# A retention block and a Strassen feed-forward: where the weight forms, their first sums and v's scaling stand in the queues

## The chip, the cores and the metric

The kernel runs on one core of a Trainium2 chip. The metric is device time in microseconds (us), lower is better. The core has five instruction queues: PE (matmul), DVE (vector), ACT (scalar), POOL (GpSimd) and SP, which here only issues transfers. ACT and POOL issue transfers too. Each queue is worked off in order.

## The reference, cut to what matters

```python
def _attn_ref(q, k, v):            # each (8, 8, 576, 64): batch, heads, sequence, head width
    scores = 1/sqrt(64) * q @ k.T
    rel = pos[:, None] - pos[None, :]
    Dmat = where(rel >= 0, gamma[:, None, None] ** rel, 0.0)   # one gamma per head
    return (scores * Dmat) @ v
...
x = attn_out.transpose(0, 2, 1, 3).reshape(4608, 512)
a = x @ w1                          # 512 -> 1024
b = x @ w2
h = a * b @ w3                      # 1024 -> 1024
out = h @ w_out                     # 1024 -> 512
```

Everything is float32. The weights arrive as float64 and are converted by hand.

## The kernel before, in words

**Attention.** The batch is worked in four pairs (`i`), and the 576 positions of a pair in five chunks, one of 64 and four of 128. So there are 20 chunks, `g` from 0 to 19. For each chunk the kernel loads k (`ld_k`) and v (`ld_v`). From the second pair on it also loads q, and a little later k, in 32 x 32 blocks (`load_blocks`, L171: sixteen transfers of 32 KB for q and sixteen for k, half as many for a short chunk), so that DVE can transpose them (`front_blocks`, L190). POOL multiplies v by the decay (`scale`, L204) and q's blocks by theirs (`scale_blocks`, L181). Then come the scores on PE (`score`, L233), their mask on DVE (L236), the running state (`state`, L255, copied by ACT in L259), and the product with v (`pv`, L274 and L299, copied by ACT into `xT` in L306).

**Feed-forward.** `w3` and `w_out` are multiplied into one matrix `w3o` early on. What remains per token is two products with `w1` and `w2` (`up`), their elementwise product (`ab`), and one product with `w3o` (`down`). Both use Strassen's scheme with seven products for eight. In `up` (L524) and `down` (L637) it is one level deep. A `down` takes two groups of 128 tokens: PE makes products 1, 7, 2, 6, 5, 4 and 3, ACT copies product 1 (L667) and product 2 on top of it (L682), and DVE makes the sums (L681, L641) and the operands S3, S2, S1, S4 (L607, L611, L613, L679). The result tile `ot` has one buffer. Its rows are stored by ACT (L708).

From token block 4 on, `up2` goes one level deeper, for two token blocks at a time (a group; there are four groups of 14 steps, seven for each half of the weights). Each step is one of the seven outer products P1, P2, P6, P7, P4, P5, P3, and makes seven inner products of 0.65 us each. It needs one set of weight forms of 896 KB, which doesn't stay on the chip: the sets are computed once by `weight_forms`, written to HBM (`kept`), and read back step by step into a ring of three slots in `ra` (`next_forms`, L931). A step issues the read for the step after the next. In a step ACT copies three or four results (L1036, L1040, L1043, L1031), POOL adds earlier results to them (`more`, L1022), DVE adds the rest (L1029, L1027), and for every second quarter of the result DVE multiplies the two factors into `ab` (L994). The last inner product of a step (`rest`) is put off into the step after it, behind that step's second product, by `finish`. The token side has sums too: `token_forms` (L940, all on POOL), once per group.

**Handing over the weights.** `wA0`, `wA1` (weights of half 0 and 1) and `wS0`, `wS1` (their sums) fill the space that the ring and the result tiles take over. `weight_forms(h, False)` makes one pair of sums on DVE (L868: one on wA, one on wS) and sends two thirds of the forms; `weight_forms(h, True)` makes three more pairs in place, and sends the rest. One half is 6.4 MB. A send is five transfers per piece (L878 of 256 KB or 128 KB each, L881 or L884 for wS), all issued by POOL. The work of these functions is put in a list, `spread`, from which `up` and `down` take one entry after each of their DVE sums. `open_first` (half 0) and `open_second` (half 1) empty the list and open the ring; `open_second` then issues the first two reads. In the third `down` of this stretch, L667 writes into `ra` as well, in the space of `wA1`.

**Order.** The order on every queue is written out by hand (`manual_schedule`); the framework adds the waits. `work(n)` takes n entries from `todo`, a list of `up`, `up2` and `down`; `aside` holds pieces (transposes, sums) that the next `up` or `down` takes along. The stretch that the change touches first is this:

```python
todo.extend([*ups[:2], forms[0], ups[2], forms[1], ups[3], forms[2], (down, (1, 0), (1, 1)), forms[3],
             (down, (2, 2), (3, 2)), (open_second,), (down, (3, 0), (3, 1))])
```

and the loop that follows it, for chunks 10 to 19, begins with

```python
scale(g + 1, "v")
work(n - 2)
scale_blocks(g + 1)
for nm in "qk":
    aside.append(lambda nm=nm: front_blocks(g + 1, nm))
    work(1)
```

where v of chunk g + 1 was asked for at the end of the turn before, on ACT's queue.

Of the kernel before, what the change touches and what calls it, by code (L numbers as in the profile page):

```python
# [19 lines left out]
def kernel(  # L20
# [13 lines left out]
    nc = tc.nc  # L34
# [590 lines left out]
    def down(x, y, then=None, last=False):  # L625
        a, done, left = pair_of(x, y)
        second = "first" in live
        ahead(x, y)
        while len(done) < (1 if second else 3):
            aside.pop(0)()  # L630
        ps = {}
        ot = pools["ot"].tile([P, 2, 2, DM // 2], F32, tag="ot", name="ot")

        def product(nm, A, B, on=None):
            ps[nm] = ps[on] if on else acc.tile([P, DM // 2], F32, tag="acc", name="po")
            for f in range(NP):
                nc.tensor.matmul(ps[nm], a[A][:, f, :], live["W"][B][:, f, :], start=(f == 0 and not on),  # L637
                                 stop=(f == NP - 1), skip_group_check=True)

        def plus(nm, to, sb):  # L640
            nc.vector.tensor_add(ot[:, to[0], to[1]], ps[nm], ot[:, sb[0], sb[1]])  # L641
            if spread:
                spread.pop(0)()
            if second and aside and nm != 3:
                aside.pop(0)()

        def put(m, t, row, half=slice(0, 2)):

            i, n = every[m]
            r0 = t * P  # L650
            while r0 < (t + 1) * P:
                b = r0 // TB
                e = min((b + 1) * TB, (t + 1) * P)
                r = (2 * i + b) * S + n * TB + r0 - b * TB
                stores.append((out[r:r + e - r0, half.start * DM // 2:half.stop * DM // 2],
                               ot[r0 - t * P:e - t * P, row, half].rearrange("p h d -> p (h d)")))
                r0 = e
            if not keep_stores and not second:
                store()

        C11, C12, C21, C22 = (0, 0), (0, 1), (1, 0), (1, 1)
        product(1, "A11", "B11")
        first = ot[:, 0, 0]
        if second:
            first = live["first"].pop(0)
            live["first"].append(first)
        nc.scalar.copy(first, ps[1])  # L667
        if second:
            store()
            finish()  # L670
        product(7, "S3", "T3")
        if second:
            multiply()
        while len(done) < 3:
            aside.pop(0)()
        if then:
            ahead(*then)
        product(2, "A12", "B21", on=1)
        nc.vector.tensor_tensor(out=a["S4"], in0=a["A12"], in1=a["S2"], op=ALU.subtract)  # L679
        product(6, "S2", "T2")  # L680
        nc.vector.tensor_add(ot[:, 0, 1], ps[6], first)  # L681
        nc.scalar.copy(ot[:, 0, 0], ps[2])  # L682
        plus(7, C21, C12)
        product(5, "S1", "T1")
        plus(5, C22, C21)
        product(4, "A22", "-T4")
        plus(4, C21, C21)
        put(*y, 1)
        if last or second:
            put(*x, 0, slice(0, 1))  # L690
        if second:
            store()
        product(3, "S4", "B22", on=5)
        while aside and not second:
            aside.pop(0)()
        plus(3, C12, C12)
        put(*x, 0, slice(1 if last or second else 0, 2))
        if last:
            store()
        while aside:  # L700
            aside.pop(0)()
# [156 lines left out]

    def weight_forms(h, second):

        wa, ws = wA[h].rearrange("p r j c n -> p (r j) c n"), wS[h]

        def tt(out, in0, in1, op):
            def both():
                for w in (wa, ws):
                    o, x, y = (w[:, :, c, m * QC:(m + 1) * QC] if w is wa else w[:, :, m, :, c, :]
                               for m, c in (out, in0, in1))
                    nc.vector.tensor_tensor(out=o, in0=x, in1=y, op=op)  # L868
            return both

        def send(pieces):
            for lo, m, c in pieces:
                n = 2 * P if c == 1 else 4 * P
                for a in range(4):
                    f, r = divmod(a, 2)
                    x = wA[h][:, r, :, :, m * QC + f * P:m * QC + f * P + P]
                    x = x.rearrange("p j c n -> p (j c) n") if c is None else x[:, :, c, :]
                    nc.gpsimd.dma_start(kept[h][a, :, lo:lo + n].rearrange("p (g n) -> p g n", n=P), x)  # L878
                to = kept[h][4:7, :, lo:lo + n].rearrange("a p n -> p a n")
                if c is None:  # L880
                    nc.gpsimd.dma_start(to, wS[h][:, :, m].rearrange("p a j c n -> p a (j c n)"))  # L881
                else:
                    for j in range(2):
                        nc.gpsimd.dma_start(to[:, :, j * P:(j + 1) * P], wS[h][:, :, m, j, c, :])  # L884

        if second:
            return [tt((1, 1), (1, 1), (1, 0), ALU.subtract), tt((0, 0), (1, 1), (0, 0), ALU.add),
                    tt((0, 1), (0, 1), (1, 1), ALU.subtract),
                    lambda: send([(8 * P, 0, None), (12 * P, 1, 1)])]
        return [tt((1, 0), (0, 0), (1, 0), ALU.subtract), lambda: send([(0, 0, None), (4 * P, 1, None)])]  # L890
# [21 lines left out]
    def open_second():  # L912
        nonlocal acc
        while spread:
            spread.pop(0)()
        acc_part.close()
        acc = ctx.enter_context(tc.tile_pool(name="acc", bufs=5, space=PSUM, reuse_waits="tile"))
        pools["seed"] = ctx.enter_context(tc.tile_pool(name="seed", bufs=2, space=PSUM, reuse_waits="tile"))
        ra = wp.tile([P, 32 * P], F32, tag="wA1", name="ra")
        cs = wp.tile([P, 2, 4, 2, TB], F32, tag="wS1", name="cc")  # L920
        ring.extend([ra[:, :FORM], ra[:, FORM:2 * FORM]])
        free.extend(cs[:, j] for j in range(2))
        live["first"] = [ra[:, 2 * FORM + j * DM // 2:2 * FORM + (j + 1) * DM // 2] for j in range(2)]
        for _ in range(2):
            next_forms()

    def next_forms():
        n = sent[0]
        if n < 14 * len(groups):
            nm = NAMES.index(OPERANDS[order[n % 7]][0])  # L930
            nc.gpsimd.dma_start(ring[n % 3], kept[n % 14 // 7][nm])  # L931
            sent[0] += 1

    def token_forms(gr):
# [5 lines left out]
            nc.gpsimd.tensor_tensor(out=out, in0=in0, in1=in1, op=op)  # L940

        for s in range(2):
            B = [[x[s][:, 2 * r:2 * r + 2, b, :] for b in range(2)] for r in range(2)]
            tt(B[0][1], B[1][1], B[0][1])
            tt(T[:, s, 1], B[0][1], B[0][0], ALU.add)
            tt(T[:, s, 0], B[1][1], T[:, s, 1])
            tt(T[:, s, 2], B[1][0], T[:, s, 1])
        b11, b21 = (x[0].rearrange("p (r c) b t -> p r c b t", c=2)[:, :, c] for c in range(2))
        b12, b22 = (x[1].rearrange("p (r c) b t -> p r c b t", c=2)[:, :, c] for c in range(2))
        tt(b12, b22, b12)  # L950
        tt(E[:, 1], b12, b11, ALU.add)
        tt(E[:, 0], b22, E[:, 1])
# [44 lines left out]
    def up2(gr, n):  # L997
# [41 lines left out]
        product(p5, "S1", "T1", True)  # L1039
        nc.scalar.copy(c[:, 3], p5)  # L1040
        finish()
        product(p6, "S2", "T2")
        nc.scalar.copy(c[:, 1], p6)  # L1043
        for o in both:
# [9 lines left out]
            more(c, add, 1)  # L1054
        for o in both:
            more(o, c, 1)
        next_forms()
        product(p6, "S3", "T3")
        plus(p6, 3, c)
        plus(p5, 1, c)  # L1060
        if both:
            multiply()
        if aside:
            aside.pop(0)()

        def rest():
# [6 lines left out]
            elif key == "P4":  # L1073
                results.append((gr, h, 1, 0, c))
            elif key == "P5":
                free.append(c)
                results.append((gr, h, 1, 1, sums2["P7"]))
            elif key == "P3":
                free.append(sums2["P6"])
# [39 lines left out]
    for g in first_pair:  # L1119
# [28 lines left out]
            scale_blocks(g + 2)  # L1148
        if g == NC + 1:
            list(strassen_tokens(1, 0))  # L1150
            forms = [(lambda h=h, second=second: spread.extend([lambda: None] * (2 * second) + weight_forms(h, second)),)
                     for h in halves for second in (False, True)]
            ups = [(up, 1, 0, fp) for fp in range(NQ)]
            todo.extend([*ups[:2], forms[0], ups[2], forms[1], ups[3], forms[2], (down, (1, 0), (1, 1)), forms[3],
                         (down, (2, 2), (3, 2)), (open_second,), (down, (3, 0), (3, 1))])
        if not in_blocks[g + 1]:
            work(n // 2)
# [9 lines left out]
    scale(g + 1, "v")  # L1167
    open_first()
    rest = token_forms(0)

    g = 2 * NC
    work(1)
# [11 lines left out]
    for g in range(2 * NC, G):  # L1184
        n = dealt[g - 2 * NC]
        if g + 1 < G:
            scale(g + 1, "v")
            work(n - 2)
            scale_blocks(g + 1)
            for nm in "qk":  # L1190
                aside.append(lambda nm=nm: front_blocks(g + 1, nm))
                work(1)
# [64 lines left out]
```

## Time and profile before

| | |
|---|---|
| median of 8 runs | 897.47 us (894.01 to 901.94) |
| the profiled execution | 898.61 us, its span from first to last instruction 896.9 us |
| mean granted PE clock | 0.977 of full speed |
| busy: PE, DVE, POOL, ACT | 829.5, 554.9, 343.5, 257.9 us |
| moved by the transfer engines | 128.77 MB, mean 144 GB/s |
| reads of weight forms (`ra<-kept`) | 56 of 896 KB, median 5.0 us from issue to landing |
| q and k blocks (`bl_q`, `bl_k`) | 408 of 32 KB, median 2.5 us |

Stages, by the timeline: the first pair with the conversion of the weights (to about 200 us), the second pair with `up` and `down` (to 320), the weights sent out between three `down` (320 to 380), then the four groups of `up2`, each followed by three `down` (from 390 to the end).

How to read it: "busy" is an engine's own work. A wait is put down to what ended last before the waiting instruction. `seed` and `up` are accumulators in PSUM; `cc` are the result tiles of the steps; "x4" behind a row of the timeline is a number of instructions merged into it. Each product in float32 shows twice as many matmul records as the code has calls. The timeline's three columns at the left are start, duration (both in us) and engine; a bracket tells the idle time before it and what ended it. In a list of waits the numbers are the sum in us, how often, and the longest.

### The profile page before, as it was taken

The numbers are of one execution on the slowest core, as the hardware profiler recorded it, in microseconds if no ns is written. First come the engines' busy times: TensorE is split into PE (matmuls) and PEld (weight loads), VectorE is DVE, ScalarE is ACT, GpSimd is POOL, SyncE is SP. The second block draws the span as 40 slices with busy tenths as digits, with TensorE's granted clock in tenths as the row PEclk, the third lists the DMA queues.
The fourth block names the chain that finished last, engine by engine and source line by source line (L and its number), as shares of the span: only waits on it lengthen the run. The fifth ranks groups of instructions, "written<-read, shape, count | busy, mean of one in ns | idle before, by whom it ended". The sixth has DMA issues, their size and how long they took to land.

```text
span 896.9 us, 15684 instructions
## 1 busy us (share of the span) xinstructions
PE 829.5 (92%) x6053; PEld 739.7 (82%) x6053; DVE 554.9 (62%) x891; ACT 257.9 (29%) x501; POOL 343.5 (38%) x349
## 2 busy tenths in 40 slices
PE   7999999999999988868988899999899999999998
PEld 6889999446889976767887688888789898898987
DVE  4989899963554665414646933667735759346563
ACT  4786566641111110022321003222013231033200
POOL 1100010002013545964446913647904458534510
PEclk8999999999999998979989999999999999999999
DMA  9994544533255687558786337587546452235401
GB/s 192 218 221 113 90 129 137 141 71 59 48 108 107 130 273 247 172 172 206 169 229 150 78 73 175 206 204 202 92 86 178 151 197 88 85 124 188 164 24 47
DMA packets 234089, 128.77 MB, mean 144 GB/s; under 512 B 203096, under 2 KB 216664, under 8 KB 234016
## 3 DMA queue, kind: packets, MB, share of 16 engines
q1 hardware_dynamic: 188448, 47.52, 27.5%
q0 software_dynamic: 11872, 64.23, 20.7%
q10 hardware_dynamic: 33696, 16.03, 7.7%
q8 instruction: 47, 0.77, 0.4%
q14 instruction: 26, 0.21, 0.1%
HBM read 105.46 MB, written 22.28 MB: 142 GB/s over the span
## 4 chain that ended last, share of the span: by engine, by line
PE 54%; DMA 20%; DVE 8%; POOL 7%; SPq 5%; issue 4%; ACT 1%; ACTq 0%; DVEq 0%; POOLq 0%
PE po L637 19%; PE up L524 9%; PE up L1017 8%; DMA ra<-kept 7%; PE ps L477 6%; PE seed L1017 6%; DMA ld_v<-in_v_dram 5%; SPq L171 4%; DMA bl_k<-in_k_dram 3%; PE sc L233 2%; DMA out_dram<-ot 2%; POOL cc L1022 2%; PE xps L299 2%; DVE ab L994 2%; DVE cc L1029 1%
## 5 line engine op out<-in xcount | busy, mean ns | idle before, releaser
L1022 POOL TENSOR_TENSOR cc<-cc 128x384 f32<-128x384 f32 x112 | 111.8, 1008 | 111.4 <-ACT cc L1040 99.6
L637 PE MATMUL po<-w3o,ab 128*128 128x256 f32 x552 | 126.0, 383 | 5.1 <-DVE ot L641 2.4
L637 PEld LDWEIGHTS po<-w3o,ab 128*128 128x128 f32 x552 | 105.3, 192 | 21.0 <-DVE ot L641 3.4
L1029 DVE TENSOR_TENSOR cc<-seed,cc 128x384 f32<-128x384 f32 x88 | 48.7, 554 | 96.5 <-PE seed L1017 90.4
L204 POOL TENSOR_TENSOR ld_v<-ld_v,gk 128x1024 f32<-128x1024 f32 (+1 forms) x18 | 34.4, 1910 | 182.4 <-DMA ld_v<-in_v_dram 171.7
L1017 PE MATMUL up<-xT,ra 128*128 128x192 f32 x384 | 76.8, 334 | 16.8 <-DMA ra<-kept 14.9
L1017 PEld LDWEIGHTS up<-xT,ra 128*128 128x128 f32 x384 | 63.8, 191 | 22.5 <-issue 10.5
L524 PE MATMUL up<-xT,wA 128*128 128x192 f32 x384 | 70.5, 327 | 0.0
L637 PE MATMUL po<-wB,forms 128*128 128x256 f32 x288 | 66.8, 385 | 3.8 <-DVE forms L611 3.3
L1036 ACT COPY seed<-up 128x384 f32<-128x384 f32 x56 | 25.9, 463 | 152.6 <-PE up L1017 128.5
L1029 DVE TENSOR_TENSOR cc<-up,cc 128x384 f32<-128x384 f32 x88 | 48.3, 549 | 31.6 <-PE up L1017 30.2
L181 POOL TENSOR_TENSOR bl_q<-bl_q,gqs 128x512 f32<-128x512 f32 (+1 forms) x30 | 31.0, 1053 | 95.1 <-DMA bl_q<-in_q_dram 89.7
L1017 PE MATMUL up<-ra 128*128 128x192 f32 x288 | 57.3, 336 | 10.7 <-DMA ra<-kept 10.6
L529 DVE TENSOR_TENSOR c<-up,c 128x384 f32<-128x384 f32 x80 | 44.0, 550 | 36.6 <-PE up L524 36.0
L637 PEld LDWEIGHTS po<-wB,forms 128*128 128x128 f32 x288 | 55.3, 193 | 12.9 <-issue 4.0
L236 DVE TENSOR_TENSOR pm<-sc,mask 128x512 f32<-128x512 f32 (+1 forms) x80 | 45.4, 628 | 31.6 <-PE sc L233 31.6
L524 PEld LDWEIGHTS up<-xT,wA 128*128 128x128 f32 x384 | 63.4, 190 | 1.2 <-issue 0.5
L1017 PEld LDWEIGHTS up<-ra 128*128 128x128 f32 x288 | 48.7, 195 | 13.8 <-DMA ra<-kept 10.4
L477 PE MATMUL ps<-wo,w3T 128*128 128x512 f32 x128 | 55.1, 592 | 0.0
L994 DVE TENSOR_TENSOR ab<-cc 128x384 f32<-128x384 f32 x64 | 54.1, 886 | 0.8
L1017 PE MATMUL seed<-e,ra 128*128 128x192 f32 x256 | 53.0, 339 | 0.5 <-DVE cc L1029 0.4
L679 DVE TENSOR_TENSOR ab<-ab,forms 128x512 f32<-128x512 f32 x17 | 16.8, 988 | 52.6 <-PE po L637 52.6
(126 smaller groups left out, 1553.8 us busy)
## 6 DMA issues: line engine op xcount, KB each, us to landing
ra<-kept POOLq DMA_DIRECT2D x56, 896.0 KB, 5.0
raw<-in_moe_w_dram SPq DMA_DIRECT2D x72, 128.0 KB, 3.0
bl_q<-in_q_dram SPq DMA_DIRECT2D x216, 32.0 KB, 2.5
ld_k<-in_k_dram SPq DMA_DIRECT2D x13, 512.0 KB, 5.3
out_dram<-ot ACTq DMA_DIRECT2D x50, 128.0 KB, 2.3
bl_k<-in_k_dram SPq DMA_DIRECT2D x192, 32.0 KB, 2.5
kept<-wA POOLq DMA_DIRECT2D x24, 256.0 KB, 4.0
ld_v<-in_v_dram ACTq DMA_DIRECT2D x11, 512.0 KB, 6.9
```

The lines of the kernel that those rows point to most:

```text
L171: nc.sync.dma_start(t[part:part + BL, :, m, :], src[a, :, s0:s0 + BL, f * BL:(f + 1) * BL].rearrange("m r x -> r m x"))
L181: nc.gpsimd.tensor_tensor(out=part, in0=part, in1=gqs[:, :, n0:n0 + n].unsqueeze(3).to_broadcast([P, NP, n, BL]), op=ALU.mult)
L204: engine.tensor_tensor(out=t, in0=t, in1=gam[:sz, c].unsqueeze(1).unsqueeze(3).to_broadcast([sz, 2, H, D]), op=ALU.mult)
L236: nc.vector.tensor_mul(pm[:sz, b, j, :, :sz], sc[j][:sz, :, :sz], mask[:sz, :sz].unsqueeze(1).to_broadcast([sz, NP, sz]))
L477: nc.tensor.matmul(ps, live["w3T", ft][:, g, :], live["wo"][:, g, :], start=(g == 0), stop=(g == KF - 1))
L524: nc.tensor.matmul(ps[:, w, :], a[:, w, r, :], b[:, r, :], start=(new and w == r == 0), stop=(w == r == 1), skip_group_check=True)
L529: nc.vector.tensor_add(c[:, to], ps, c[:, sb])
L637: nc.tensor.matmul(ps[nm], a[A][:, f, :], live["W"][B][:, f, :], start=(f == 0 and not on), stop=(f == NP - 1), skip_group_check=True)
L994: nc.vector.tensor_mul(ab, v[:, :, 0, :], v[:, :, 1, :])
L1017: nc.tensor.matmul(ps[:, w, :], weight_of(slot, a, w), B[b], start=(new and w == 0), stop=True, skip_group_check=True)
L1022: nc.gpsimd.tensor_tensor(out=o, in0=o, in1=i, op=ALU.add)
L1029: nc.vector.tensor_add(c[:, j], ps, with_add[:, j])
```

## The change

Six edits. (1) The order of the weight forms: half 0's first sums stay where they are, half 1's first sums and half 0's second sums both come after the last `up`, during the first `down`, and half 1's second sums are put in `spread` behind `token_forms(0)`, so that the second `down` takes them. (2) The sends of half 1's second forms, and the two reads of `open_second`, are issued by SP instead of POOL. (3) In `token_forms` the sums of the two token blocks alternate, with both first sums ahead. (4) `next_forms` moves in a step from behind POOL's adds to directly behind `finish()`. (5) The P5 step gives its own tile `c` back before `multiply`, and not in its `rest`. (6) In the loop v is scaled behind q's blocks; and in one `down` (g == 2 * NC - 1) the first half of a row is stored before product 3, as is done later on.

```diff
@@ down
-        if last or second:
+        early = second or last or g == 2 * NC - 1
+        if early:
             put(*x, 0, slice(0, 1))
...
-        put(*x, 0, slice(1 if last or second else 0, 2))
+        put(*x, 0, slice(1 if early else 0, 2))
@@ weight_forms
+        engine = nc.sync if h and second else nc.gpsimd
...
-                    nc.gpsimd.dma_start(kept[h][a, :, lo:lo + n].rearrange("p (g n) -> p g n", n=P), x)
+                    engine.dma_start(kept[h][a, :, lo:lo + n].rearrange("p (g n) -> p g n", n=P), x)
...
@@ open_second, next_forms
         for _ in range(2):
-            next_forms()
+            next_forms(nc.sync)
...
-    def next_forms():
+    def next_forms(engine=nc.gpsimd):
...
-            nc.gpsimd.dma_start(ring[n % 3], kept[n % 14 // 7][nm])
+            engine.dma_start(ring[n % 3], kept[n % 14 // 7][nm])
@@ token_forms
         for s in range(2):
-            B = [[x[s][:, 2 * r:2 * r + 2, b, :] for b in range(2)] for r in range(2)]
-            tt(B[0][1], B[1][1], B[0][1])
-            tt(T[:, s, 1], B[0][1], B[0][0], ALU.add)
-            tt(T[:, s, 0], B[1][1], T[:, s, 1])
-            tt(T[:, s, 2], B[1][0], T[:, s, 1])
+            tt(x[s][:, :2, 1], x[s][:, 2:, 1], x[s][:, :2, 1])
...
+        sums = [(T[:, s, 1], x[s][:, :2, 1], x[s][:, :2, 0], ALU.add) for s in range(2)]
+        sums += [(T[:, s, 0], x[s][:, 2:, 1], T[:, s, 1]) for s in range(2)]
+        sums += [(T[:, s, 2], x[s][:, 2:, 0], T[:, s, 1]) for s in range(2)]
+        for args in sums:
+            tt(*args)
@@ up2
         finish()
+        next_forms()
         product(p6, "S2", "T2")
...
-        next_forms()
         product(p6, "S3", "T3")
         plus(p6, 3, c)
         plus(p5, 1, c)
         if both:
+            free.append(c)
             multiply()
...
             elif key == "P5":
-                free.append(c)
                 results.append((gr, h, 1, 1, sums2["P7"]))
@@ the second pair
-            forms = [(lambda h=h, second=second: spread.extend([lambda: None] * (2 * second) + weight_forms(h, second)),)
+            forms = [(lambda h=h, second=second: spread.extend(weight_forms(h, second)),)
                      for h in halves for second in (False, True)]
...
-            todo.extend([*ups[:2], forms[0], ups[2], forms[1], ups[3], forms[2], (down, (1, 0), (1, 1)), forms[3],
+            todo.extend([*ups[:2], forms[0], *ups[2:], forms[2], forms[1], (down, (1, 0), (1, 1)),
                          (down, (2, 2), (3, 2)), (open_second,), (down, (3, 0), (3, 1))])
...
     open_first()
     rest = token_forms(0)
+    spread.extend(weight_forms(1, True))
@@ the loop
-            scale(g + 1, "v")
             work(n - 2)
             scale_blocks(g + 1)
+            scale(g + 1, "v")
```

More of the change, by code (lines that the diff above doesn't have):

```diff
@@ L877, in send @@
                     x = x.rearrange("p j c n -> p (j c) n") if c is None else x[:, :, c, :]
-                    nc.gpsimd.dma_start(kept[h][a, :, lo:lo + n].rearrange("p (g n) -> p g n", n=P), x)
+                    engine.dma_start(kept[h][a, :, lo:lo + n].rearrange("p (g n) -> p g n", n=P), x)
                 to = kept[h][4:7, :, lo:lo + n].rearrange("a p n -> p a n")
                 if c is None:
-                    nc.gpsimd.dma_start(to, wS[h][:, :, m].rearrange("p a j c n -> p a (j c n)"))
+                    engine.dma_start(to, wS[h][:, :, m].rearrange("p a j c n -> p a (j c n)"))
                 else:
                     for j in range(2):
-                        nc.gpsimd.dma_start(to[:, :, j * P:(j + 1) * P], wS[h][:, :, m, j, c, :])
+                        engine.dma_start(to[:, :, j * P:(j + 1) * P], wS[h][:, :, m, j, c, :])
         if second:
```

## The prediction

> **What bounds the kernel now.** I read the page's slices first, then the list of waits, then the timelines of PE, POOL and SP around the longest waits. PE is busy 829.5 of 896.9 us, so what can be won is PE's idle time and the slow matmuls after it.
>
> ```profile
> PE   7999999999999988868988899999899999999998
> PEclk8999999999999998979989999999999999999999
> DMA  9994544533255687558786337587546452235401
> ```
>
> A slice is 22.4 us. PE falls below nine tenths in slices 15 to 22 (about 314 to 515 us), and there the granted clock falls too. After that it is nearly full. The list of waits, first of the whole span, then of SP between 390 and 405 us:
>
> ```profile
> PE up L1017 <- DMA ra<-kept: 25.5, 14, 10.0
> PE po L637 <- ACT ot L667: 4.1, 1, 4.1
> POOL ld_v L204 <- DMA ld_v<-in_v_dram: 171.7, 12, 42.3
> POOL kept L878 <- DVE wA L868: 22.9, 2, 13.0
> DVE wA L868 <- DMA kept<-wA: 11.0, 2, 7.9
> ...
> SPq L171 <- DMA out_dram<-ot: 13.3, 1, 13.3
> ```
>
> PE waits 25.5 us for weight forms, 10.0 of it once. POOL, which issues those loads, stands 171.7 us in L204 waiting for v, with the loads queued behind it. The timeline of POOL shows both:
>
> ```profile
> 364.78 1.01 POOL L940 TENSOR_TENSOR xT<-xT 128x384 f32<-128x384 f32 x1
> ...
> 384.13 1.13 POOL L940 TENSOR_TENSOR u<-ra,u 128x192 f32<-128x192 f32 x2
> 385.21 1.13 POOL L931 DMA_DIRECT2D ra<-kept  x2
> ...
> 445.52 1.89 POOL L204 TENSOR_TENSOR ld_v<-ld_v,gk 128x1024 f32<-128x1024 f32 x1 [10.78 <-PE up L1017]
> 447.37 0.59 POOL L931 DMA_DIRECT2D ra<-kept  x1
> ```
>
> The first forms are issued only after 20.4 us of token sums (L940). Later, a load goes out at 447.4, behind the scaling of v. PE's timeline shows the price:
>
> ```profile
> 390.13 1.62 PE L1017 MATMUL up<-xT,ra 128*128 128x192 f32 x4 [9.96 <-DMA ra<-kept]
> 452.97 1.65 PE L1017 MATMUL up<-ra 128*128 128x192 f32 x4 [3.69 <-DMA ra<-kept]
> 459.90 0.81 PE L1017 MATMUL seed<-ra 128*128 128x192 f32 x4
> ```
>
> After a long wait four matmuls take 1.65 us instead of 0.81: a second price of a stall, worth 2.0 us at 390, 3.0 at 453 and 3.0 at 350.
>
> **What the Trainium skill says.** "TensorE: Matmul & The Clock Gate", Part 1, says that an idle PE is clocked at half rate until about 3.4 us of activity. The trace agrees (1.65 against 0.81; some 5 us at half rate cost 2 to 3). "SBUF — State Buffer", Who interferes with whom, says that a DVE tensor_tensor with both inputs in SBUF contends with GpSimd's reads. The trace agrees: two L994 took 3.97 us beside L940 at 500.8, and 1.02 at 403.6. "DMA: Bandwidth & Descriptors", Issuing engines are not separate DMA queues, says that issuing from another engine saves only issue time. So I give SP's sends no more bandwidth than POOL's had (2.69 MB from 356.7 to 366.2).
>
> **The change part by part.** The 896 KB forms take 5.0 us to land; a step of seven products takes 4.55 us on PE (0.65 each).
>
> *Part 1, spilling the weights (320 to 390 us).* Before, three pairs of L868 (1.22+0.95 us) sat in the last `up`, and DVE came late: PE waited 0.37 and 1.91 us, then ran 24 matmuls in 6.93 us instead of 5.45. The pairs leave, so the first `down` starts at 323.4 instead of 326.2 and ends near 335.8 instead of 340.0. Half 1's first forms are sent there from about 333 by POOL (ten sends of 0.75 us); half 0's second set follows to about 352. The early put splits one 256 KB store in two of 128 KB, but L667 of the next `down` waits for the whole buffer and thus for both. With 6.3 MB of sends beside it, I put that at 346 instead of 350.3; PE still stalls and runs cold (3.0 us).
> The second sums of half 1 now come in the second `down`, after product 6 (about 353). Three pairs are 6.5 us, but POOL's L940 now runs beside them; I add 3 us by the L994 row. So they end at 362.5, against 357.2 before. SP then issues eleven sends; I take 8.5 us to landing, 371, against POOL's 9.5. SP's issue of such a send is not in the trace: its 32 KB loads take 0.31 to 0.84 us, POOL's send 0.75, so eleven cost 3.4 to 9 us, and I use 6. Behind them on SP stand only the two form loads and the blocks of chunk 11; the fourth k block waits, before and after, for a store of step 0 with which it shares a completion semaphore (the 13.3 us above), so these blocks move with step 0, and their scores wait about 1 us as before. The third `down` writes its first copy (L667) into the place of those weights, and waits for them: at 371.4 against 366.6. That is a new PE wait of some 8 us, and a cold start. Five products (8.65), 2.7 for the cold and 3.5 for state, scores and seed give step 0 at 386.2, against 390.13. The form loads no longer matter: SP issues the first at 369, landing at 374. POOL's sums start at 352, wait for half 0's sends until 356, and have E by 369. So the stall moves from ra<-kept to L667. Gain 3.9, and 2.0 for the cold start at 390 that moved: **5.9 us**. Bounds: 12 if the sends land at 366, a loss of 4 if they land at 381.
>
> *Part 2, v scaled after q's blocks.* In the loop POOL no longer stands behind v's load with adds and forms behind it. PE waits 2.42 (423), 3.69 with 3.0 cold (453), and 2.47 with some 2.5 cold (479.6; a sum on DVE that waited for POOL): 14 us in all. Not all comes back. SP issues 16+16 block loads and one of 512 KB per chunk in about 26 us: from 403.9 to 430.3, then 432.8 to 458.6. PE needs 4 x 4.55 + 6.2 = 24.4 us for a chunk of four steps. SP was idle 2.5 and 4.6 us between those runs. That is 7.1 us, and then SP's loads (kT L190, L233) are the bound; I take **6**. The scale itself (1.9 us) is late for nobody: state and pv come two steps later. It does stand ahead of the next form load, which goes out some 4 us into its step there, as every load does now.
>
> *Part 3, the next form ahead of the adds.* Today the load is issued after the two L1022, about 4.1 us into a step, and lands 9.1 to 10 us in; it is needed at 9.1. It moves behind the wait for the last product of the step before (1.95 us in), about 2.1 us earlier. Waits after 510 us are 1.74, 0.25, 1.08, 0.69, 0.36, 0.69, 0.92, 0.58, 1.53 and 0.65, together 8.5. I take **6**, since 2 stay where the scalings precede the load. The adds come about 0.6 us later on POOL; their reader is the L1029 after the last product but one, which at 4.5 us still finds them done in ordinary steps and is some 0.5 us late in the fifth.
>
> *Part 4.* The token sums are the same 8 L940 in another order, so nothing; they lie beside PE's work except in part 1. The fifth product's tile, read last by POOL about 2 us into the next step, replaces one that L994 had just multiplied: PE's waits for L1040 are 1.6 us in all, and I take **0.5**.
>
> **Sum.** 5.9 + 6 + 6 + 0.5 = 18.4. The profiled execution took 898.6 us (span 896.9 and 1.7 around it), 1.1 above the median of 897.5: 880.2 by that execution, about 879.5 beside the median. Half a per cent, 4.5 us, is about what a measurement of this kernel can tell from no change.
>
> **Rivals.**
> *Transfers take it back* (0.18). DMA share is already 0.80 to 0.82 between 410 and 470. If forms, sends and blocks only shift, part 1 gives 2, part 2 nothing and part 3 gives 4: 891. For it: SP's near-continuous run of loads. Against: SP was idle 7.1 us, and waits after 510 come at a DMA share of 0.45 to 0.76.
> *Everything goes* (0.13). The sends land by 366, PE stays warm through the third `down`, and parts 2 and 3 give 14 and 8: 12 + 14 + 8 = 34 less some 2 left over, 866. Against: the order of DVE's sums puts the sends after product 6.
> *Slower: the load at the head of POOL's queue* (0.13). It waits for PE to leave the slot, and the adds wait behind it. If they then set PE's pace, each of 56 steps loses the 0.57 us of the issue: 32 us, less 18 won, gives 911. It decides once the adds end later than 4.5 us into a step; I have them at 4.55. For it: POOL's 343.5 us, which cluster in the steps. Against: PE waits only 2.9 us for L1029 now, and `acc` has five buffers, so a late add holds a sum, not the next product.
> That the change does not do what it says I hold likely only for the early put.
>
> **Numbers.** Forecast 0.56 around 879.5 (868 to 888 by its own bounds). The range 866 to 894 takes in the first two rivals and leaves out the third and a tail. Faster by over 0.5% are the forecast, "everything goes" and most of the first rival: 0.80. Within 0.5%: 0.07. Slower: 0.13.
>
> **What would show it.** In the profile after: no long wait of PE for ra<-kept near 390, and L667 of the third `down` waiting for kept near 371 instead; no wait of POOL in L204 ahead of L931; ra<-kept waits after 510 under 3 us together; the block loads of SP almost without gaps from 400 to 480. I am wrong if PE's waits for ra<-kept stay above 10 us, or if waits for POOL's adds grow past 5.

## The result, and the profile after

The changed kernel takes 909.1 us in the median, against 896.4 for the kernel before beside it: a ratio of 1.0143, 95% interval 1.0121 to 1.0165. So it is slower by 12.7 us where 18 us less were forecast. The profiled execution has a span of 906.5 us (896.9 before) and a mean granted clock of 0.968 (0.977).

The slices of the kernel after, 22.7 us each:

```profile
PE   8899999999999995987988999797999799998998
PEclk7999999999999998899898999898999899999999
```

PE now falls to seven tenths in slices 26, 28 and 32 (around 575, 624 and 714 us), where it had been nearly full, and the clock falls there too. The list of PE's waits from 380 us to the end (us in total, how often, longest), after:

```profile
PE sc L233 <- DVE kT L190: 19.1, 6, 5.4
PE seed L1021 <- DVE cc L1033: 13.6, 11, 2.3
PE seed L1021 <- DVE cc L1031: 12.5, 6, 6.1
```

The same list of the kernel before began like this (L1017 there is L1021 here, L1027 and L1029 are L1031 and L1033):

```profile
PE up L1017 <- DMA ra<-kept: 25.5, 14, 10.0
PE sc L233 <- DVE kT L190: 7.1, 5, 2.2
...
PE seed L1017 <- DVE cc L1029: 2.9, 2, 2.5
```

The 25.5 us of waits for weight forms are gone altogether. In their place PE waits for DVE: for the sums of the steps, and for kT, the transposed blocks of k. By stages, from the timeline of PE, each from its first product, or from the end of the `down` before it, to the first product of the `down` behind it, in us:

| | before | after |
|---|---|---|
| step 0 starts | 390.1 us | 381.5 us |
| group 0, to its first `down` | 109.8 | 109.5 |
| group 1, behind group 0's `down` | 89.2 | 98.7 |
| group 2 | 82.1 | 92.5 |
| group 3 (no chunk of the attention left) | 69.1 | 68.6 |

At 500 us the new kernel is still 9 us ahead. Group 0 takes as long as before, because a gain and a loss cancel there: waits for forms behind step 0 (7.0 us) are gone, and 11.7 us of waits for the sums L1031 and L1033 have come. Groups 1 and 2 lose some 20 us. Between 500 and 760 us, PE's waits for kT grow from 3.6 to 14.2 us, those for the sums from nothing to 9.7, three blocks of scores (L233) run at half rate, 1.7 us longer each, and 5.7 us of waits for forms are gone. Group 3 has the same 14 steps but no attention in it, and loses nothing.

What happens in groups 1 and 2 is seen at the end of the P5 step near 565 us. DVE in the kernel after:

```profile
566.69 0.56 DVE L1031 TENSOR_TENSOR cc<-up,cc 128x384 f32<-128x384 f32 x1 [0.39 <-POOL cc L1026]
567.16 2.90 DVE L998 TENSOR_TENSOR ab<-cc 128x384 f32<-128x384 f32 x2
569.99 1.23 DVE L190 STREAM_TRANSPOSE qT<-bl_q 128x1024 f32<-128x1024 f32 x1
...
574.50 1.23 DVE L190 STREAM_TRANSPOSE kT<-bl_k 128x1024 f32<-128x1024 f32 x1
```

POOL in the same kernel and stretch:

```profile
558.33 2.05 POOL L181 TENSOR_TENSOR bl_q<-bl_q,gqs 128x512 f32<-128x512 f32 x2
560.35 1.89 POOL L204 TENSOR_TENSOR ld_v<-ld_v,gk 128x1024 f32<-128x1024 f32 x1
562.20 0.59 POOL L934 DMA_DIRECT2D ra<-kept  x1
562.81 3.85 POOL L1026 TENSOR_TENSOR cc<-cc 128x384 f32<-128x384 f32 x4
566.62 0.57 POOL L934 DMA_DIRECT2D ra<-kept  x1
567.21 1.95 POOL L1026 TENSOR_TENSOR cc<-cc 128x384 f32<-128x384 f32 x2
```

Read them together. The two scalings and the form stand ahead of P5's four adds, so these end at 566.7. DVE's last sums wait for them one by one (0.39 us each). Then DVE multiplies (L998) at the same moment as POOL begins the next step's two adds: two multiplications take 2.90 us, while two of them elsewhere take 1.03. The transposes are queued behind. The same place in the kernel before, DVE and then POOL, whose adds begin only when the multiplications are done:

```profile
575.10 1.02 DVE L994 TENSOR_TENSOR ab<-cc 128x384 f32<-128x384 f32 x2
```

```profile
576.78 1.95 POOL L1022 TENSOR_TENSOR cc<-cc 128x384 f32<-128x384 f32 x2 [1.64 <-ACT cc L1040]
```

PE's timeline shows the end of it, first before and then after:

```profile
582.31 2.06 PE L233 MATMUL sc<-qT,kT 64*128 64x128 f32 x32 [1.84 <-DVE kT L190]
```

```profile
575.88 3.79 PE L233 MATMUL sc<-qT,kT 64*128 64x128 f32 x32 [4.79 <-DVE kT L190]
```

In the kernel after, PE waits 4.79 us and then runs the scores at half rate (3.79 us against 2.06). The group of L998 shows how much longer the multiplications take over the whole run; the last number before the second bar is the mean in ns. Before (L994) and after:

```profile
L994 DVE TENSOR_TENSOR ab<-cc 128x384 f32<-128x384 f32 x64 | 54.1, 886 | 0.8
```

```profile
L998 DVE TENSOR_TENSOR ab<-cc 128x384 f32<-128x384 f32 x64 | 71.8, 1161 | 0.8
```

### The profile page after: what moved, and what is told of

Read it like the earlier page. It is cut to its first block, busy times and chain, and to the rows that moved or that the text cites. A ratio compares the mean times of both kernels' runs of the same rounds, so it can differ in the third digit from the quotient of the medians.

```text
span 906.5 us, 15699 instructions
## 1 busy us (share of the span) xinstructions
PE 830.9 (92%) x6053; PEld 745.1 (82%) x6053; DVE 579.6 (64%) x891; ACT 258.3 (28%) x501; POOL 337.2 (37%) x336
## 3 DMA queue, kind: packets, MB, share of 16 engines
q0 software_dynamic: 10736, 59.64, 19.1%
## 4 chain that ended last, share of the span: by engine, by line
PE 56%; DVE 12%; DMA 10%; issue 9%; POOL 8%; SPq 4%; ACT 1%; DVEq 0%; ACTq 0%; POOLq 0%
PE po L637 20%; PE up L524 10%; PE up L1021 7%; PE ps L477 6%; PE seed L1021 6%; POOL cc L1026 5%; DVE ab L998 3%; DMA ld_v<-in_v_dram 3%; PE sc L233 3%; SPq L171 3%; PE xps L299 2%; DMA bl_k<-in_k_dram 2%; DVE cc L1033 2%; DMA bl_q<-in_q_dram 1%; DMA out_dram<-ot 1%
## 5 line engine op out<-in xcount | busy, mean ns | idle before, releaser
L637 PE MATMUL po<-w3o,ab 128*128 128x256 f32 x552 | 128.1, 387 | 12.5 <-DVE ot L641 11.1
L1026 POOL TENSOR_TENSOR cc<-cc 128x384 f32<-128x384 f32 x112 | 110.0, 1007 | 3.8 <-ACT cc L1044 2.4
L934 POOL DMA_DIRECT2D ra<-kept x54 | 30.7, 568 | 209.9 <-PE seed L1021 208.2
L1033 DVE TENSOR_TENSOR cc<-seed,cc 128x384 f32<-128x384 f32 x88 | 48.7, 554 | 69.3 <-PE seed L1021 61.0
L1021 PE MATMUL up<-xT,ra 128*128 128x192 f32 x384 | 76.6, 337 | 0.6 <-ACT cc L1044 0.6
L998 DVE TENSOR_TENSOR ab<-cc 128x384 f32<-128x384 f32 x64 | 71.8, 1161 | 0.8
L181 POOL TENSOR_TENSOR bl_q<-bl_q,gqs 128x512 f32<-128x512 f32 (+1 forms) x30 | 30.9, 1050 | 104.5 <-DMA bl_q<-in_q_dram 89.9
L204 POOL TENSOR_TENSOR ld_v<-ld_v,gk 128x1024 f32<-128x1024 f32 (+1 forms) x18 | 34.4, 1912 | 91.4 <-DMA ld_v<-in_v_dram 90.8
L1021 PEld LDWEIGHTS up<-xT,ra 128*128 128x128 f32 x384 | 66.2, 196 | 2.2 <-ACT cc L1044 0.9
L1033 DVE TENSOR_TENSOR cc<-up,cc 128x384 f32<-128x384 f32 x88 | 48.3, 549 | 30.5 <-PE up L1021 29.8
L233 PE MATMUL sc<-qT,kT 64*128 64x128 f32 (+1 forms) x640 | 45.3, 301 | 21.7 <-DVE kT L190 19.1
L1040 ACT COPY seed<-up 128x384 f32<-128x384 f32 x56 | 25.9, 463 | 137.1 <-PE up L1021 93.1
L233 PEld LDWEIGHTS sc<-qT,kT 64*128 64x128 f32 (+1 forms) x640 | 41.4, 209 | 24.2 <-issue 19.1
L1021 PE MATMUL seed<-e,ra 128*128 128x192 f32 x256 | 52.5, 337 | 7.1 <-DVE cc L1033 7.1
L1021 PE MATMUL seed<-u,ra 128*128 128x192 f32 x192 | 40.0, 339 | 18.9 <-DVE cc L1031 12.5
```

The costliest lines, as they stand in the source:

```text
L181: nc.gpsimd.tensor_tensor(out=part, in0=part, in1=gqs[:, :, n0:n0 + n].unsqueeze(3).to_broadcast([P, NP, n, BL]), op=ALU.mult)
L204: engine.tensor_tensor(out=t, in0=t, in1=gam[:sz, c].unsqueeze(1).unsqueeze(3).to_broadcast([sz, 2, H, D]), op=ALU.mult)
L233: nc.tensor.matmul(sc[j][:sz, p, :sz], kT[hs, b, p, :sz], qT[hs, b, p, :sz], start=True, stop=True)
L998: nc.vector.tensor_mul(ab, v[:, :, 0, :], v[:, :, 1, :])
L1021: nc.tensor.matmul(ps[:, w, :], weight_of(slot, a, w), B[b], start=(new and w == 0), stop=True, skip_group_check=True)
L1026: nc.gpsimd.tensor_tensor(out=o, in0=o, in1=i, op=ALU.add)
```

## The experiments

Twelve kernels ran. The first four take edits of the change back, three of them one edit each. The theory at that point was POOL's queue: adds late behind the form load and the scalings, and nothing else. Its rivals were v alone, the tile of P5, and the weights' order.

**v at the head of the loop again.** The edit, in the loop of the kernel after:

```diff
+            scale(g + 1, "v")
             work(n - 2)
             scale_blocks(g + 1)
-            scale(g + 1, "v")
```

> The kernel after, with v scaled at the head of the loop again, as before the change; all else as after. Theory (the queue of POOL): the slower P5 steps come from two things in front of POOL's four adds, the form load at the head (0.59 us, and its wait for PE) and the two scalings (2.05 for the blocks, 1.89 for v). Taking v away shortens the queue by 1.9 us in ten chunks, but the waits for v come back: about 900 us. Rival (v alone): the scaling of v in front of the adds is the whole loss: 889 us. Rival (tile of P5): no difference, 909 us. Rival (weights' new order loses later what it wins): 907 us.

Measured: 907.5 us, ratio to the kernel before 1.0112 (1.0066 to 1.0159). Neither the theory (900) nor v alone (889) is right: taking the 1.9 us away hardly helps. The two rivals that expected no effect, the weights' order (907) and the tile (909), lie next to it.

**The form behind the adds again.**

```diff
         finish()
-        next_forms()
         product(p6, "S2", "T2")
...
             more(o, c, 1)
+        next_forms()
         product(p6, "S3", "T3")
```

> The kernel after, with the next form issued behind POOL's adds again; all else as after. Theory (the queue of POOL): POOL's adds no longer stand behind the load's wait for PE, so PE's waits for L1031 and L1033 (26 us in the profile after) shrink to under 6 us and those for kT to about 10; some waits for forms come back: about 895 us. Rival (v alone): v's 1.89 us stay in front of the adds, little changes: 906 us. Rival (tile of P5): 908 us. Rival (weights' order): 907 us.

Measured: 902.8 us, 1.0068 (1.0044 to 1.0092). Half of the loss goes, less than the theory said. The wait for the P5 sums near 480 us is still 6.00 us. There the scalings keep the adds late without the form, mostly because they start late: POOL waits 6.26 us for the blocks ahead of L181, and the two scalings then take 3.9 us.

**P5's tile given back late again.**

```diff
         if both:
-            free.append(c)
             multiply()
...
             elif key == "P5":
+                free.append(c)
                 results.append((gr, h, 1, 1, sums2["P7"]))
```

> The kernel after, with the tile of P5 given back in its put-off part again; all else as after. Theory (the queue of POOL): the tile is read last by POOL's adds of the same step, so ACT's copy in the P3 step (10.1 us of waits, but PE waits 0.6 for it) costs little: about 908 us. Rival (tile of P5): this coupling is what hands POOL's delay to PE: 895 us.

Measured: 894.9 us, 0.9978 (0.9959 to 0.9997). The theory fell here: it gave 908. This one line is worth 14 us, and the kernel is then as fast as the one before. But the rival's reason (ACT's copy waits for POOL and hands the delay on) isn't what the traces show either. Here are DVE, ACT and POOL in the same place of this kernel:

```profile
568.07 0.56 DVE L1031 TENSOR_TENSOR cc<-up,cc 128x384 f32<-128x384 f32 x1 [0.39 <-POOL cc L1026]
568.55 1.02 DVE L998 TENSOR_TENSOR ab<-cc 128x384 f32<-128x384 f32 x2
569.48 1.24 DVE L190 STREAM_TRANSPOSE qT<-bl_q 128x1024 f32<-128x1024 f32 x1
```

```profile
569.65 0.48 ACT L1044 COPY cc<-up 128x384 f32<-128x384 f32 x1 [4.45 <-DVE ab L998]
```

```profile
570.22 1.95 POOL L1026 TENSOR_TENSOR cc<-cc 128x384 f32<-128x384 f32 x2 [1.65 <-ACT cc L1044]
```

POOL's adds are as late as before the edit: DVE's last P5 sum still waits 0.39 us for them. But the P3 step now takes the tile that has just been multiplied. So ACT's copy waits for L998, POOL's next adds wait for the copy, and L998 is over before they begin: 1.02 us instead of 2.90. PE pays 1.18 us for ACT's copy, and its wait for kT is 1.84 instead of 4.79. In the kernel after, ACT's copy needs only P5's own tile, and POOL goes on at once. The wait that the edit removes had kept two engines apart.

**v and the form back, the tile early.** Both edits above that touch v and the form, together.

> The kernel after, with both v scaled at the head of the loop and the next form behind the adds, so that the new order of the weights, the order of the token sums and P5's tile are what is left of the change. Theory (the queue of POOL): the 9 us that step 0 starts earlier are kept: 888 us. Rival (weights' order): step 0 starts earlier, but the chunks' blocks come no earlier, and it is given back by 700 us: 897 us, or with the loss in it 905 us. Rival (tile of P5): 900 us or more.

Measured: 888.4 us, 0.9882 (0.9835 to 0.9928). With v and the form where they were, the early tile does no harm, and the new order of the weights keeps its gain to the end.

From this came a second theory, **a lost order**: late adds on POOL (from the form, the scalings, or both) and the early tile are needed together; the multiplication then stands beside POOL's adds, and the transposes behind it are late. The next four do single edits on the kernel before.

> The kernel before, with P5's tile given back before the multiplication, and nothing else changed. Theory (a lost order): the tile that the P3 step got before was the one just multiplied, so ACT's copies, and with them POOL's next two adds, came behind the multiplication on DVE; with P5's own tile they no longer do, and the adds run beside it. It costs only where POOL's adds of P5 are late. In the kernel before they end about as PE's products do, so this alone gives 897 us, 0 to 4 above the kernel before, and L994 stays near 0.9 us. Rival (fewer waits for ACT's copies): 0.5 to 2 us faster, 895. Rival (the tile is bad by itself, wherever POOL stands): 14 us slower as in the changed kernel, 910.

Measured: 896.7 us, 0.9992 (0.9976 to 1.0008). L994 stays at 887 ns. As the theory said, the tile alone does nothing that can be told from zero; the gain of 0.5 to 2 us that the first rival gave lies within the interval and isn't excluded.

> The kernel before, with the next form issued directly behind the put-off product, ahead of POOL's adds, and nothing else changed. Theory (POOL's adds behind the form): waits for forms vanish after 510 us (8.5 us), waits for L1029 and L1027 come in their place, 0.8 us in seven steps and 1 to 2 in the P5 steps: 896 us, within 3 of the kernel before. Rival (the loads gain as forecast): 890 us. Rival (the head of the queue costs by itself): 905 us.

Measured: 895.7 us, 0.9983 (0.9966 to 1.0000). PE's waits for forms fall from 25.5 to 10.7 us in the profile, 8.2 of them at step 0, and waits for L1029, L1027 and L1040 grow from 4.8 to 17.8. So the form early is a trade, not a gain. The mean of L994 is 1029 ns here (886 before), and the kernel is no slower for it: a stretched multiplication costs only where something that PE needs stands behind it.

> The kernel before, with v scaled behind q's blocks in the loop, and nothing else changed. Theory (POOL's adds behind two scalings): the waits for v (PE waits 2.4, 3.7 and 2.5 us between 420 and 480, and the cold clock behind two of them) go, but 1.9 us stand in front of P5's adds in ten chunks: 897 us, from 893 to 901. Rival (forecast): 890 us.

Measured: 900.2 us, 1.0041 (1.0021 to 1.0061), at the high end of what the theory gave. POOL and PE of this kernel:

```profile
478.46 2.06 POOL L181 TENSOR_TENSOR bl_q<-bl_q,gqs 128x512 f32<-128x512 f32 x2 [6.92 <-DMA bl_k<-in_k_dram]
480.49 1.89 POOL L204 TENSOR_TENSOR ld_v<-ld_v,gk 128x1024 f32<-128x1024 f32 x1
482.35 3.84 POOL L1022 TENSOR_TENSOR cc<-cc 128x384 f32<-128x384 f32 x4
```

```profile
484.93 1.65 PE L1017 MATMUL seed<-u,ra 128*128 128x192 f32 x4 [6.43 <-DVE cc L1027]
```

POOL waits 6.92 us ahead of L181 (the trace names a transfer of k's blocks as the last to come), scales q's blocks, scales v, and only then makes P5's adds; PE waits 6.43 us for the sum behind them and runs on at half rate.

> The kernel before with the new order of the weight forms, their sends and the first two reads by SP, the early half row and the new order of the token sums; form load, v and P5's tile as before. Theory: the start of step 0 at about 381 us instead of 390 is kept to the end: 887 us. Rival (tile early helps where POOL is not late): 890 us, above the kernel that has the tile early as well (888). Rival (transfers take it back): 893 us.

Measured: 890.5 us, 0.9909 (0.9881 to 0.9937): 8 us won, as much as step 0 starts earlier (382.0 us, against 390.1). The 890 of the rival "tile early helps where POOL is not late" is nearest; the theory (887) and "transfers take it back" (893) both lie about 3 us off. Whether the early tile adds something here isn't shown: the intervals of 0.9909 and of 0.9882, the same kernel with the early tile, overlap.

The last four put the second theory to the test. **The two harmless edits together**, form and tile, on the kernel before:

> The kernel before with two edits, each of which alone changed nothing that can be told: the next form ahead of POOL's adds, and P5's tile given back before the multiplication. Theory (a lost order): the form makes POOL's adds of P5 late, and with P5's own tile the next step's adds are no longer kept behind the multiplication, so they run beside it: L994 goes to about 1.15 us in the mean, PE's waits for kT to 19 us: 909 us, from 905 to 914. Rival (the edits add up): 895 us.

Measured: 918.1 us, 1.0243 (1.0214 to 1.0271). Two edits that alone make 0.9992 and 0.9983 cost 2.4% together, 22 us, more than the theory gave (909, at most 914). Six of the ten blocks of scores run slow, at 3.08 to 3.79 us; in the kernel before it is one, with the tile alone three, with the form alone one. PE's waits for kT from 380 us on, and the group of L994:

```profile
PE sc L233 <- DVE kT L190: 24.0, 6, 6.2
```

```profile
L994 DVE TENSOR_TENSOR ab<-cc 128x384 f32<-128x384 f32 x64 | 78.5, 1266 | 0.8
```

**The multiplication moved, the tile left early.** This undoes nothing of the change; it only takes L998 out of the place where it collides.

```diff
         if both:
             free.append(c)
-            multiply()
```

> The kernel after, with the multiplication of the P5 step (two L998) moved on DVE behind the next step's first two sums, where that step multiplies anyway; tiles, form and v as in after. Theory (a lost order): the two L998 no longer stand beside POOL's adds (two of 0.98 us, which start as the P5 sums end), so L998 falls from 1.16 us in the mean to 0.95 or less and PE's waits for kT from 19 to about 10: 898 us, from 894 to 902. Rival (the tile itself: ACT's copy of the P3 step waits for POOL's adds): the tiles are the same, nothing changes: 908 us.

Measured: 897.8 us, 1.0014 (0.9994 to 1.0034), against 1.0143 for the kernel after. DVE and POOL in the same place:

```profile
567.15 1.24 DVE L190 STREAM_TRANSPOSE qT<-bl_q 128x1024 f32<-128x1024 f32 x1
568.31 0.99 DVE L1031 TENSOR_TENSOR cc<-seed,cc 128x384 f32<-128x384 f32 x2
569.22 1.95 DVE L998 TENSOR_TENSOR ab<-cc 128x384 f32<-128x384 f32 x4
...
572.48 1.24 DVE L190 STREAM_TRANSPOSE kT<-bl_k 128x1024 f32<-128x1024 f32 x1
```

```profile
567.20 1.97 POOL L1026 TENSOR_TENSOR cc<-cc 128x384 f32<-128x384 f32 x2
```

The transpose of q and two sums now fill the 1.97 us of POOL's adds, and four multiplications behind them take 1.95 us. P5's sums end at the same 567.2 us as in the kernel after, but kT's transpose starts 2.0 us earlier, and PE's waits for kT are 9.8 us instead of 19.1. The same instructions stand ahead of that transpose in both kernels, four L998 among them: these take 2.90 + 1.03 us there and 1.95 here, which is the whole 2.0 us. So it isn't a shorter queue that helps, but a queue in which no multiplication stands beside POOL's adds. The tiles and POOL's queue are those of the kernel after, and 11 us of its loss are gone. The mean of L998 is 1000 ns, a little above the 950 expected; pairs of 3.11 us are left, at 545.93 us for instance, with no transpose close behind them.

**The form early, the tile late, v first**, with the weights' order:

> The kernel after, with P5's tile late and v at the head of the loop, so that the weights' order and the early form are what is left. Theory (a lost order): without the early tile the early form is about neutral, as it was alone: 889 us, from 886 to 893. Rival (the early form costs once the start is earlier, since the chain of POOL's adds is then the bound): 897 us.

Measured: 888.5 us, 0.9922 (0.9893 to 0.9950), as the theory said.

**The early form issued by ACT**, with the weights' order, the early tile and v first:

```diff
         finish()
-        next_forms()
+        next_forms(nc.scalar)
         product(p6, "S2", "T2")
```

> The weights' order and P5's tile as after, v at the head of the loop, and the next form issued as early as in after, but by ACT, behind its copies, so that POOL's adds don't stand behind it. Theory (a lost order): what made the early form costly is that POOL's adds wait behind it, not the earlier transfer; without that no L998 is stretched, forms still come early: 886 us, from 883 to 890. Rival (the earlier transfers themselves press on the chunks' blocks): 900 us or more.

Measured: 883.2 us, 0.9859 (0.9818 to 0.9900): the lowest median of all, and clearly below both kernels; from the kernel with v and the form back (0.9882, 0.9835 to 0.9928) it can't be told apart. It differs from the v-at-the-head kernel (907.5 us) in this one word. So it isn't the earlier transfer that costs, but what stands behind it in POOL's queue. POOL waits for the slot to come free and then takes 0.57 to 0.59 us for the issue (ACT 0.33); which of the two weighs more was not separated. No wait of PE for forms is left from 380 us on, and L998 takes 738 ns in the mean, less than in the kernel before (886). PE's three largest sums of waits are then these; the last of them, for ACT, is the price:

```profile
PE sc L233 <- DVE kT L190: 12.5, 6, 3.6
PE po L637 <- DVE ot L641: 3.9, 3, 1.9
PE seed L1021 <- ACT cc L1048: 3.7, 5, 1.3
```

The ratios of the kernels that have each edit on or off, beside each other ("weights" is the new order with SP's sends, the early half row and the order of the token sums):

| weights | form early | v last | tile early | ratio to before |
|---|---|---|---|---|
| - | - | - | yes | 0.9992 |
| - | yes | - | - | 0.9983 |
| - | - | yes | - | 1.0041 |
| - | yes | - | yes | 1.0243 |
| yes | - | - | - | 0.9909 |
| yes | - | - | yes | 0.9882 |
| yes | yes | - | - | 0.9922 |
| yes | yes | yes | - | 0.9978 |
| yes | - | yes | yes | 1.0068 |
| yes | yes | - | yes | 1.0112 |
| yes | yes | yes | yes | 1.0143 |

## Why the prediction was wrong, point by point

The four parts alone sum to 0.9909, 0.9992, 0.9983 and 1.0041, thus 0.75% or 6.7 us faster; 18.4 were forecast. That is the smaller error. The larger is that they do not add: the whole is 12.7 us slower, so 19 us come from edits acting on each other. The prediction did look at v's scaling ahead of the form, but nowhere at the early tile together with adds that come later. That is the step that failed: later adds were held to be harmless and the early tile to be a pure gain, and the two together cost 22 us on the kernel before (1.0243).

*Part 1 (5.9 us forecast): right in the amount, if a little small, but not in what holds PE.* Alone it won 8 us (5.6 to 10.7). Step 0 starts at 381.5 us, not 386.2. Three pairs of L871 took 9.7 us beside POOL's sums, as forecast (9.5), but began at 348.9 and not at 353; that start is the mis-sized term. The second `down`'s copy (L667) came at 343.9 instead of 346, and after a wait of 1.74 us PE was not cold there, where the forecast had put 3.0 us for it. From the end of the sums to the copy L667 there were 8.4 us, against 8.5 in the forecast. SP's eleven sends were issued from 357.3 to 364.3, 7 us where 6 were taken. SP's timeline after:

```profile
357.26 2.19 SPq L881 DMA_DIRECT2D kept<-wA  x4
359.55 0.53 SPq L884 DMA_DIRECT2D kept<-wS  x1
360.12 3.04 SPq L881 DMA_DIRECT2D kept<-wA  x4
363.20 1.09 SPq L887 DMA_DIRECT2D kept<-wS  x2
364.60 2.59 SPq L934 DMA_DIRECT2D ra<-kept  x2
```

The stall did move into the third `down`, but not to L667. Two timelines, PE and then ACT:

```profile
363.49 7.75 PE L637 MATMUL po<-w3o,ab 128*128 128x256 f32 x24 [10.10 <-DVE ot L641]
```

```profile
367.31 0.37 ACT L667 COPY ra<-po 128x256 f32<-128x256 f32 x1 [18.35 <-DMA kept<-wS]
```

PE stood for a sum, L641, that was queued on DVE behind the weights' sums and the operands of the `down`, and was cold after it. L667 waited 18.35 us, and PE did not wait for it.

*Part 2 (6 us forecast): the wrong sign.* Alone it loses 3.7 us (1.9 to 5.5). The waits for v do go. The step that failed is "the scale itself (1.9 us) is late for nobody": it was followed to v's readers, and to the form, but not to P5's four adds behind it in the same queue, and the sum behind the adds held PE for 6.43 us. v's 1.89 us are the smaller part of that: POOL had waited 6.92 us ahead of L181 for the blocks, a wait that the prediction priced only at kT and the scores. Nor are 171.7 us of waiting for v what it seemed to be: only 79.1 of them fall behind 380 us, where there are loads of forms to hold up.

*Part 3 (6 us forecast): 1.5 us (0 to 3).* The waits for forms go, as was said. The sentence that the adds would still be done in ordinary steps failed: in the kernel with this edit alone, PE waited 7.3 us in ten places for L1029 (2.9 in two before), many of them 0.83 us, and 6.0 us for L1040 (1.6 before).

*Part 4 (0.5 us forecast): right alone, 0.7 us with an interval from -0.7 to 2.2, and the decisive mistake in company.* The edit was costed only by a wait that it removes. That this wait (ACT's copy behind L994) also held POOL's next adds back until the multiplication was done was not asked. The prediction had the price in hand, from the Trainium skill, "SBUF — State Buffer", Who interferes with whom (a DVE tensor_tensor with both inputs in SBUF contends with GpSimd's reads), and had found two L994 at 3.97 us beside L940. It used it in part 1 and not here. The runs agree with that page: L998, with both inputs in SBUF, took 2.90 us for two beside L1026 and 1.02 without it; L1031, whose first input is in PSUM, took 0.56 us beside L1026.

*The rivals.* "Slower: the load at the head of POOL's queue" gave 911 and lies nearest, and its place was right: issued by ACT, the same early load costs nothing. Its working was not. It charges 0.57 us to each of 56 steps, but group 3, with 14 such steps, loses nothing (68.6 against 69.1 us), and the early form alone is neutral. In group 3 two L998 at the end of a P5 step take 3.09 us as well (826.75), with no transpose behind them. What the prediction held against this rival failed too: "`acc` has five buffers, so a late add holds a sum, not the next product". All of PE's waits for L1031 and L1033 (26.1 us in 17 places, against 3.2 in three before) stand in front of products into `seed`, not into `acc`: the late sum must have read `seed` before the put-off product adds to it. What decides is the end of the P5 steps in groups with attention, and only with the early tile. "Transfers take it back" and "everything goes" are refuted by the same table.

*The signs named beforehand.* No long wait for forms near 390 us, no wait of POOL in L204 from 380 us on, waits for forms after 510 us under 3 us (none): these came true, as did the wait of L667 for `kept`, and the kernel was slower all the same. One sign failed: SP's block loads almost without gaps from 400 to 480 us. SP stood idle 5.8 us from 420.6 and 6.9 from 446.9, longer than the 2.5 and 4.6 before, mostly waiting for DVE's transpose of q. Buffers that came free late, and not SP's own pace, held the loads there, which part 2 had not reckoned with. The one that gave the alarm was the last: waits for POOL's adds beyond 5 us. They were seen as DVE's: `L1031` waited 14.8 us for L1026, and PE 26.1 us for L1031 and L1033.

Two small readings of the prediction were off as well: the stretch from 314 to 515 us is slices 15 to 23, and the half rate behind the stall at 453 us lasted over 5 us, which is longer than the 3.4 us that the prediction said it agreed with.

Open is how the 22 us of form and tile together divide between L998 itself, the clock behind each stall, and blocks that are asked for later in consequence (the stretch isn't the same everywhere: at 578 us in that kernel the two L994 take 1.82 us, at 620 us 4.93); and why they weigh less with v late in the whole change than the sum of the single ratios says.

## What to carry to other kernels

When an edit frees a buffer earlier, ask not only who waited for it, but which two instructions that wait kept from running at the same time: here a copy that waited for a multiplication also kept POOL's adds away from it. Price the edits of a change in pairs where they touch the same few microseconds of a step: two that each made no difference cost 2.4% together. And when a load is to go out early, issue it from a queue with nothing urgent behind it; between POOL and ACT, the same load in the same place of the step made a difference of some 23 us (1.0112 against 0.9859).

## What was not expected of the hardware

The collision is not shared out evenly. Around 567 us in the kernel after, POOL's two adds took 1.95 us, as they do without L998, and only DVE was stretched (2.90 us for two, about as long as both kinds of work one after the other: 1.02 + 1.95). With v and the form back, two L998 at 560.8 us took 1.82 us and POOL's two adds 2.63. ACT issues the 896 KB load in 0.33 us, POOL in 0.57 to 0.59. And a wait of some 2.5 us can be enough for half rate, or not: after 2.47 us at 468.2 in the fastest kernel eight matmuls took 2.70 us (1.46 elsewhere), while after 2.94 us at 401.6 in the kernel with v and the form back the scores took their usual 2.06. The same scores near 570 us took 3.55 us after a wait of 2.79 with the multiplication moved, and 2.06 after 2.75 with v and the form back. So the length of the wait alone doesn't decide.
